# An attention and feed-forward kernel on one Trainium2 core: splitting the values by a fixed power of two, checking them by products with themselves, and judging the range early

## The chip, the cores and the metric

One core of a Trainium2 chip. The metric is the device time of one launch in microseconds. The program has five engines that run side by side and meet by semaphores: TensorE (PE, with its weight loads as PEld), VectorE (DVE), ScalarE (ACT), GpSimd (POOL) and SyncE (SP), which issues the DMAs.

## What is computed

Three steps, all from float32 inputs except the weights of the second and third, which come as float64.

```python
# 1. attention: batch 2, 8 heads, 768 positions, head size 64
scores = q @ k.T / 8 - slope[h] * dist
keep = (col < n_global) | ((0 <= row - col) & (row - col < n_local))   # 8 and 96 here
a = exp(where(keep, scores, -1e9) - max);  a = a / (sum(a) + 1e-9)
x = a @ v                                     # heads side by side: 2 x 768 x 512
# 2. h = relu(x @ w_in) (512 -> 1024), a 3-tap convolution along the positions per channel
x = (h * sigmoid(conv(h))) @ w_out            # 1024 -> 512
# 3. h = relu(x @ w_in) (512 -> 1024), u, v = halves of h; v normalised over channels
v_s = w_spatial @ v_n + b_spatial             # over the 768 positions
out = (u * v_s) @ w_out                       # 512 -> 512
```

## The kernel before, in words

Only a band of the attention is computed: 32 global columns and 96 earlier positions beside each block of 128 queries. It is right for counts within the band's reach and for numbers within the reach of float16. So the kernel computes the whole result by this banded way, gathers a flag that tells whether counts and sizes were within reach, and at its end each engine reads the flag (L1574) and branches (L1577) over a second, dense way that would compute all anew.

The positions are 6 groups (2 batches x 3 chunks of 256), each with 4 pairs of heads. A float32 operand is split into a high half (float16, scaled by a power of two, `HALF`) and a low half (what the high half left out), and a product of two such operands is three float16 matmuls: high x high, high x low, low x high (L1081 and L1151 for the second step, L1226, L1299, L1331 and L1361 for the third). In groups 0 and 1 (`PLAINS`) the values of the attention are used as they are, in float32 matmuls (L957). In groups 2 to 5 they are split: `v_scale` finds the largest absolute value of the group (`largest`, L757: a reduction over up to 1536 columns on VectorE), turns that column into a row on TensorE (L776), reduces it and makes two powers of two from its exponent in four integer steps (`scale`, L760 to L769), spreads them over the partitions by a matmul with ones (L783), and copies them out of PSUM into `cs` (L787). `v_split` then makes the high half on ScalarE (L809) and the low half on VectorE (L814), both with `cs` as a pointer operand. `weigh` uses the halves in three float16 matmuls per block (L963 to L965), and its `norm` scales back with the second power in `cs` (L969). The largest values are kept in `top`.

`watch` squares a float16 tile on ScalarE and sums it per partition into one column of `seen` (L505). Watched are x, the gated hidden blocks (`inner`, the first of 8 feature blocks of each group), ys, the weights, and the gated blocks of the third step, 61 in all. `decide` sums `seen` over the partitions with one matmul (L517), and `judge` compares each of the 61 sums with `LEAST` and `MOST`, and the largest of `top` with `MOST_X`, into the flag, in eight VectorE instructions (L526 to L533).

The order of the work is planned when the program is built. Each piece is added to `Plan` with its cost per engine it may run on, what it reads and what it writes. `order` first gives each task a time by which it is due, counted back from the end (`chain`, later `justified`), and then lists the tasks greedily (`trial`): on each engine the task that can start soonest, and of several the one that is due first; a task with two engines in its costs goes to the one that would end it sooner, within margins. PSUM banks are given out in that order too: a bank is taken at a piece's first task and comes free after its last. Six such trials are made and the shortest is taken. Each engine's instructions are then fixed in that order. A tile with fewer buffers than uses makes the later use wait for all of the earlier one (`make_room`): the raw values `v` have one buffer, their halves `vh` and `vl` two.

The lead (`tick`) goes through the steps of the attention: in the third step of a group the values of the next are loaded (`v_load`), in the sixth they are scaled, in the seventh they are split. The second step's work (`half_slot`) is added between the ticks. The third step follows (`second`), with `decide` after the last `spatial` and before the last two `last`, in the order of adding; the plan decides where they come to lie. `last` ends with evictions on ScalarE (L476) and output DMAs (L543).

Of the kernel before, what the change touches and what calls it, by code (L numbers as in the profile page):

```python
# [48 lines left out]

HALF = dict(w=8, x=11, h=12, y=12, g=12, v=8, s=16)  # L50
LEAST, MOST = 2.0e4, 4.0e9

MOST_X = 29.0

# [22 lines left out]
def dve(n):  # L77
    return 0.07 + 0.00104 * n
# [283 lines left out]
class Kernel:  # L362
    def __init__(self, ctx, tc, vb, qk, qf, kf, vf, nw, w1, cw, w2, w3u, w3v, wst, bsp, w4, out):
# [16 lines left out]
        self.craw = tile("craw", [P, 24, 2], I32)  # L380
        self.beyond = tile("beyond", [P, 4])
        self.seen = tile("seen", [P, 64])
# [3 lines left out]
        self.top = tile("top", [1, GROUPS])  # L386
        self.ng, self.nl = self.cnt[:, 0:1], self.cnt[:, 1:2]
# [21 lines left out]
            ("vl", 2 * H * D, 2), ("qk", CH + KW, 3), ("qh", CH + KW, 2), ("sb", 512, 3), ("ph", 1024, 2),  # L409
            ("pt", 1024, 2), ("xk", 2 * P, 2), ("nm", 2, 6), ("nb", 2, 6), ("r", 4, 4), ("cs", 2, 3),  # L410
            ("row", 4, 1), ("vm", 1, 1),
        )
# [98 lines left out]
    def decide(self):  # L511

        nc, n = self.nc, self.watched
        acc = self.plan.next("ps")
        self.plan.add(
            dict(PE=0.2),
            lambda e: nc.tensor.matmul(  # L517
                self.ps(acc)[:1, :n], self.column, self.seen[:, :n], start=True, stop=True
            ),
            reads=[("seen", j) for j in range(n)] + [("ident", 0)], writes=[acc],  # L520
        )

# [41 lines left out]
    def setup(self):  # L564
# [14 lines left out]
        def basics(e):  # L579
            make_identity(nc, self.ident)  # L580
            nc.gpsimd.memset(self.ones, 1.0)
            nc.gpsimd.memset(self.shift, LN2_14)
            nc.gpsimd.memset(self.column, 1.0)
            nc.gpsimd.memset(self.top, 0.0)

# [51 lines left out]
    def setup_rest(self):  # L637
# [7 lines left out]
        def flags(e):  # L645
            for j, (x, at, op) in enumerate(
                ((self.ng, float(G), ALU.is_gt), (self.nl, float(MAX_LOCAL), ALU.is_gt), (self.nl, 1.0, ALU.is_lt))
            ):
                nc.vector.tensor_scalar(
                    out=self.beyond[:, j : j + 1], in0=x, scalar1=at, scalar2=None, op0=op  # L650
                )
# [92 lines left out]

    def v_scale(self, g):
        if g in PLAINS:
            return
        nc, add = self.nc, self.plan.add
        n = 2 if g % NCH == 0 else 3
        v = self.m("v")[:, : n * 512]  # L750
        m = self.m("vm")
        row = self.m("row")[:1].bitcast(I32)
        cs = self.m("cs", g)
        top = self.top[:, g : g + 1]

        def largest(e):
            nc.vector.tensor_reduce(out=m, in_=v, axis=AX.X, op=ALU.max, apply_absolute_value=True)  # L757

        def scale(e):
            nc.vector.tensor_reduce(out=top, in_=self.ps(t)[:1, :P], axis=AX.X, op=ALU.max)  # L760
            nc.vector.tensor_scalar(
                out=row[:, 1:2], in0=top.bitcast(I32), scalar1=0x7F800000, scalar2=None, op0=ALU.bitwise_and
            )
            nc.vector.tensor_scalar(
                out=row[:, 1:2], in0=row[:, 1:2], scalar1=float(40 << 23), scalar2=-1.0,
                op0=ALU.max, op1=ALU.mult,
            )
            for j, power in ((2, 267), (3, 267 - HALF["x"])):
                nc.vector.tensor_scalar(  # L769
                    out=row[:, j : j + 1], in0=row[:, 1:2], scalar1=float(power << 23), scalar2=None, op0=ALU.add  # L770
                )

        t = self.plan.next("ps")
        add(dict(DVE=dve(n * 512)), largest, reads=[("v", g)], writes=[("vm", g)])
        add(
            dict(PE=0.12), lambda e: nc.tensor.transpose(self.ps(t)[:1, :P], m, self.ident),  # L776
            reads=[("vm", g), ("ident", 0)], writes=[t],
        )
        add(dict(DVE=0.9), scale, reads=[t, ("ident", 0)], writes=[("row", g), ("top", g)])
        t2 = self.plan.next("ps")  # L780
        add(
            dict(PE=0.05),
            lambda e: nc.tensor.matmul(self.ps(t2)[:, 0:2], self.ones, row.bitcast(F32)[:, 2:4], start=True, stop=True),  # L783
            reads=[("row", g), ("ident", 0)], writes=[t2],
        )
        add(
            dict(DVE=0.07), lambda e: nc.vector.tensor_copy(out=cs, in_=self.ps(t2)[:, 0:2]), reads=[t2],  # L787
            writes=[("cs", g)],
        )

    def v_halves(self, g):
# [3 lines left out]

    def v_split(self, g):
        if g in PLAINS:
            return
        nc, add = self.nc, self.plan.add
        cs = self.m("cs", g)  # L800
# [6 lines left out]
        def hi(e):  # L807
            if e == "ACT":
                nc.scalar.activation(out=vh, in_=v, func=AF.Copy, scale=cs[:, 0:1])  # L809
            else:  # L810
                nc.vector.tensor_scalar(out=vh, in0=v, scalar1=cs[:, 0:1], scalar2=None, op0=ALU.mult)

        def lo(e):
            nc.vector.scalar_tensor_tensor(  # L814
                out=vl, in0=v, scalar=cs[:, 0:1], in1=vh, op0=ALU.mult, op1=ALU.subtract
            )

        add(dict(ACT=act(n * 512)), hi, reads=[("v", g), ("cs", g)], writes=[("vh", g, "v")])
        add(
            dict(DVE=dve(n * 512)), lo, reads=[("v", g), ("cs", g), ("vh", g, "v")], writes=[("vl", g, "v")]  # L820
        )

# [109 lines left out]
    def weigh(self, u):  # L932
# [50 lines left out]
        )  # L983
        add(dict(DVE=1.0), norm, reads=[acc] + [("cs", g)] * (not plain), writes=[("r", u), ("xk", u)])

# [34 lines left out]
    def tick(self, more=True):  # L1020
# [5 lines left out]
        if s is not None:  # L1026
# [38 lines left out]
    def inner(self, g, f):  # L1065
# [363 lines left out]
    def banded(self):  # L1429
# [6 lines left out]
        for n in range(LEAD_TICKS):  # L1436
            if n == 2:
                self.v_scale(0)
                self.v_split(0)
# [129 lines left out]
def build(tc, *args):  # L1569
    with ExitStack() as ctx:  # L1570
        k = Kernel(ctx, tc, *args)
        k.banded()
        why = "0 or 1, whether a count or a size is beyond the reach of the banded way"
        beyond = k.nc.values_load(  # L1574
            k.flag[:1, :1], min_val=0, max_val=1, skip_runtime_bounds_check_because=why
        )
        with tc.If(beyond != 0):  # L1577
            k.dense()
# [58 lines left out]
```

## Time and profile before

| | us |
|---|---|
| median of three runs | 386.78 (386.24 to 386.82) |
| the profiled execution's own time | 385.59 |
| its span, first to last instruction | 383.7 |
| TensorE busy, share of the span | 358.4, 93% |
| VectorE busy | 277.9, 72% |
| ScalarE busy | 268.4, 70% |
| GpSimd busy | 154.7, 40% |
| mean granted clock of TensorE | 0.987 of full speed |

The profiled execution is one of the program's executions, with its own time; what a view says adds up to its span, and 1.9 us lie around that. The busy time of an engine is the union of its instructions from start to end; matmuls overlap, so the step from one start to the next tells what one costs in a stream, not its length. Branches, register reads and semaphores count as busy time nowhere, and are found under their line.

### The profile page before, as it was taken

How to read it: one execution, taken by the hardware profiler on the slowest of the kernel's cores; microseconds unless marked ns; L12 is line 12 of the kernel's file. 1: busy time of each engine (PE TensorE's matmuls, PEld its weight loads, DVE VectorE, ACT ScalarE, POOL GpSimd, SP SyncE). 2: the span in 40 equal slices, each digit the busy share in tenths (PEclk: the TensorE clock that was granted, in tenths of full speed). 3: DMA queues.
4: the chain of work that ended last, by engine and by line, in shares of the span. 5: the costliest groups of instructions: out<-in, count | busy, mean ns of one | idle time of the engine just before them, and what ended most of it. 6: DMA issues, size and time to landing. Idle time of an engine off the chain costs nothing.

```text
span 383.7 us, 7835 instructions
## 1 busy us (share of the span) xinstructions
PE 358.4 (93%) x2852; PEld 252.6 (66%) x2852; DVE 277.9 (72%) x715; ACT 268.4 (70%) x659; POOL 154.7 (40%) x225
## 2 busy tenths in 40 slices
PE   8998788789899999989899999999999999999992
PEld 5777575557778888868689766765456665555541
DVE  5799999998997899999996399881667354241501
ACT  4989797788967999898795499789947434242420
POOL 5254426895778587569653054030205100000000
PEclk9999999899999999999899999999999999999998
DMA  7979523293849557883657000450200000102021
GB/s 221 407 238 296 186 68 91 49 217 109 186 99 240 150 135 128 223 200 57 97 116 297 2 2 0 126 164 2 94 1 2 0 2 15 68 3 81 2 109 64
DMA packets 46254, 43.60 MB, mean 114 GB/s; under 512 B 34816, under 2 KB 36608, under 8 KB 45696
## 3 DMA queue, kind: packets, MB, share of 16 engines
q1 hardware_dynamic: 46208, 43.03, 40.7%
q8 instruction: 24, 0.39, 0.4%
q14 instruction: 22, 0.18, 0.1%
HBM read 31.48 MB, written 3.15 MB: 90 GB/s over the span
## 4 chain that ended last, share of the span: by engine, by line
PE 61%; DVE 21%; ACT 6%; issue 5%; DMA 3%; POOL 2%; SPq 0%; DVEq 0%; POOLq 0%
PE bank L1331 12%; PE bank L1151 10%; PE bank L1081 9%; PE bank L1299 8%; PE bank L1361 8%; PE bank L1226 8%; DVE bank L1094 4%; DVE wk_dt_float L677 3%; DVE sb_dt_float L871 3%; DVE wk_dt_float L682 2%; PE bank L852 2%; DVE wk_dt_float L674 2%; DVE ac_dt_float L1119 2%; ACT sb_dt_float L889 1%; DMA raw_dt_float<-in_w3v 1%
## 5 line engine op out<-in xcount | busy, mean ns | idle before, releaser
L1081 PE MATMUL bank<-x_dt_float,w1h_dt_float 128*128 128x260 f16 (+1 forms) x384 | 65.5, 273 | 5.7 <-DVE xk_dt_float L974 2.5
L1151 PE MATMUL bank<-hh_dt_float,w2l_dt_float 128*128 128x254 f16 (+2 forms) x192 | 53.6, 279 | 1.1 <-POOL w2l_dt_float L492 1.1
L1151 PE MATMUL bank<-hh_dt_float,w2h_dt_float 128*128 128x254 f16 (+2 forms) x192 | 53.8, 280 | 0.2 <-DVE ac_dt_float L1119 0.2
L1151 PE MATMUL bank<-hl_dt_float,w2h_dt_float 128*128 128x254 f16 (+2 forms) x192 | 53.5, 279 | 0.0
L1081 PE MATMUL bank<-x_dt_float,w1l_dt_float 128*128 128x260 f16 (+1 forms) x192 | 52.4, 273 | 0.0
L1094 DVE SCALAR_TENSOR_TENSOR bank<-hp_dt_float,cwt,bank 128x254 f32<-128x254 f32 (+2 forms) x96 | 46.2, 486 | 6.4 <-ACT bank L1088 3.6
L1331 PE MATMUL bank<-ws_dt_float,vn_dt_float 128*128 128x384 f16 x288 | 47.3, 326 | 0.0
L1081 PEld LDWEIGHTS <-w1h_dt_float 128*128 128x128 f16 x384 | 36.6, 97 | 13.2 <-issue 7.6
L492 POOL TENSOR_TENSOR hl_dt_float<-ac_dt_float,hh_dt_float 128x254 f16<-128x254 f32 (+2 forms) x47 | 33.8, 727 | 24.3 <-ACT hh_dt_float L478 21.0
L492 POOL TENSOR_TENSOR ph_dt_float<-sb_dt_float,ph_dt_float 128x512 f16<-128x512 f32 x30 | 38.4, 1283 | 11.6 <-ACT ph_dt_float L478 8.5
L1151 PEld LDWEIGHTS <-w2h_dt_float 128*128 128x128 f16 x384 | 37.0, 100 | 7.3 <-issue 0.7
L1331 PEld LDWEIGHTS <-vn_dt_float 128*128 128x128 f16 x288 | 28.2, 98 | 18.8
L871 DVE CUSTOM_DVE_ANT_0 sb_dt_float<-bank,bias_dt_float 128x256 f32<-128x256 f32 (+1 forms) x96 | 35.0, 401 | 4.7 <-POOL qk_dt_float32r L492 1.7
L889 ACT ACTIVATE sb_dt_float<-sb_dt_float,nb_dt_float 128x256 f32<-128x256 f32 (+1 forms) x64 | 29.6, 493 | 10.5 <-POOL nb_dt_float L884 9.1
L478 ACT CAST g_dt_float<-bank 128x384 f16<-128x384 f32 x16 | 7.7, 479 | 33.8 <-DVE bank L1338 33.8
L1299 PE MATMUL bank<-ys_dt_float,w3uh_dt_float 128*128 128x384 f16 x128 | 31.2, 326 | 0.0
L1335 DVE SCALAR_TENSOR_TENSOR bank<-bank,bb_dt_float 128x384 f32<-128x384 f32 x16 | 9.1, 567 | 29.1 <-PE bank L1331 29.1
L1361 PE MATMUL bank<-w4h_dt_float,g_dt_float 128*128 128x512 f16 (+1 forms) x104 | 28.8, 363 | 0.0
L1226 PE MATMUL bank<-w3vh_dt_float,ys_dt_float 128*128 128x512 f16 x96 | 28.6, 379 | 0.0
L1361 PEld LDWEIGHTS <-g_dt_float 128*128 128x128 f16 x156 | 15.2, 98 | 15.8
L677 DVE SCALAR_TENSOR_TENSOR wk_dt_float<-raw_dt_float,wk_dt_float 128x512 int32<-128x512 int32 x28 | 24.9, 898 | 0.1
L1226 PEld LDWEIGHTS <-ys_dt_float 128*128 128x128 f16 x144 | 14.1, 98 | 15.6
(172 smaller groups left out, 894.0 us busy)
## 6 DMA issues: line engine op xcount, KB each, us to landing
raw_dt_float<-in_w SPq DMA_DIRECT2D x20, 512.0 KB, 5.4
qk_dt_float<-in_qk SPq DMA_DIRECT2D x24, 336.0 KB, 3.9
v_dt_float<-in_vb SPq DMA_DIRECT2D x4, 1024.0 KB, 5.7
out_x<-wk_dt_float SPq DMA_DIRECT2D x11, 256.0 KB, 2.0
raw_dt_float<-in_wst SPq DMA_DIRECT2D x6, 384.0 KB, 4.4
raw_dt_float<-in_w3v SPq DMA_DIRECT2D x4, 512.0 KB, 5.2
raw_dt_float<-in_w3u SPq DMA_DIRECT2D x4, 512.0 KB, 6.3
v_dt_float<-in_vb SPq DMA_DIRECT2D x2, 768.0 KB, 5.9
```

Source lines behind the costliest of these rows:

```text
L492: self.engines[e].tensor_tensor(out=out, in0=in0, in1=in1, op=ALU.subtract)
L677: nc.vector.scalar_tensor_tensor(out=fi, in0=lo, scalar=29, in1=fi, op0=ALU.logical_shift_right, op1=ALU.bitwise_or)
L871: nc.vector.tensor_tensor_reduce(out=sb[:, h, :n], in0=self.ps(self.sp[s][h])[:, :n], in1=self.m("bias", 2 * p + h)[:, t0 : t0 + n], scale ...
L889: nc.scalar.activation(out=sb[:, h, :n], in_=sb[:, h, :n], func=AF.Exp, scale=-1.0, bias=nb[:, h : h + 1])
L1081: nc.tensor.matmul(self.ps(acc)[:, :nx], w[f][:, k * P : (k + 1) * P], x[:, k, x0:], start=k == n == 0, stop=k == 3 and n == 2,)
L1094: nc.vector.scalar_tensor_tensor(out=ac(), in0=near(j), scalar=tap(j), in1=ac(), op0=ALU.mult, op1=ALU.add)
L1151: nc.tensor.matmul(ps(), w[2 * d + k // 4][:, k % 4 * P : (k % 4 + 1) * P], x, start=k == n == 0, stop=k == 7 and n == 2,)
L1226: nc.tensor.matmul(ps(), x[:, y, k, tk], w[k], start=n == 0, stop=n == 11)
L1299: nc.tensor.matmul(ps(), w[e4][:, k * P : (k + 1) * P], x[:, y, k, s], start=n == 0, stop=n == 11)
L1331: nc.tensor.matmul(ps(), v[:, k, x, ek], w[:, k, s], start=n == 0, stop=n == 17)
L1335: nc.vector.scalar_tensor_tensor(out=ps(), in0=ps(), scalar=2.0 ** -(self.k["v"] + self.k["s"]), in1=bb, op0=ALU.mult, op1=ALU.add)
L1361: nc.tensor.matmul(ps(), x[:, y, k, tk], w[k][:, at], start=n == 0, stop=n == 11)
```

## The change

`v_scale` goes, with its call and its tiles `cs`, `row`, and `top`. `v_split` uses the same helper as all other splits (`parts`), with the fixed power of two of `HALF["x"]`, now 9 in place of 11: the high half may go to ScalarE or VectorE, the low half to VectorE. A new `watch_values` multiplies each 128 x 128 block of the high half with itself on TensorE, 12 blocks in group 3 and 16 in groups 2, 4 and 5, all summed in one PSUM bank, and takes the diagonal with the identity on VectorE, summed into a column of `seen`. `norm` has constants for both of its scalars. The gated hidden blocks are watched in the first chunk of each batch alone, twice in place of six times, so that `seen` has 61 columns as before. `judge` has four instructions instead of eight, its planned cost is 6.0 us in place of 1.0, and the flag has the opposite sense.

```diff
-HALF = dict(w=8, x=11, h=12, y=12, g=12, v=8, s=16)
+HALF = dict(w=8, x=9, h=12, y=12, g=12, v=8, s=16)
...
         def judge(e):
-            sums, fit, top = self.ps(acc)[:1, :n], self.m("vm")[:1], self.top
-            good = self.m("junk")[:1, :n]
+            sums, good = self.ps(acc)[:1, :n], self.m("junk")[:1, :n]
             nc.vector.tensor_scalar(out=good, in0=sums, scalar1=LEAST, scalar2=None, op0=ALU.is_ge)
             nc.vector.scalar_tensor_tensor(out=good, in0=sums, scalar=MOST, in1=good, op0=ALU.is_le, op1=ALU.mult)
-            nc.vector.tensor_reduce(out=fit, in_=good, axis=AX.X, op=ALU.min)
-            nc.vector.tensor_scalar(out=self.beyond[:1, 3:4], in0=fit, scalar1=0.5, scalar2=None, op0=ALU.is_lt)
-            nc.vector.tensor_reduce(out=fit, in_=top, axis=AX.X, op=ALU.max)
-            nc.vector.tensor_scalar(out=fit, in0=fit, scalar1=MOST_X, scalar2=None, op0=ALU.is_gt)
-            nc.vector.tensor_tensor(out=self.beyond[:1, 3:4], in0=self.beyond[:1, 3:4], in1=fit, op=ALU.max)
-            nc.vector.tensor_reduce(out=self.flag[:1], in_=self.beyond[:1], axis=AX.X, op=ALU.max)
+            nc.vector.tensor_reduce(out=self.within[:1, 3:4], in_=good, axis=AX.X, op=ALU.min)
+            nc.vector.tensor_reduce(out=self.flag[:1], in_=self.within[:1], axis=AX.X, op=ALU.min)
...
-        self.plan.add(
-            dict(DVE=1.0), judge, reads=[acc, ("flag", 0)] + [("top", g) for g in range(GROUPS)],
-            writes=[("junk", 0), ("vm", GROUPS)],
-        )
+        self.plan.add(dict(DVE=6.0), judge, reads=[acc, ("flag", 0)], writes=[("junk", 0)])
...
-        add(dict(ACT=act(n * 512)), hi, reads=[("v", g), ("cs", g)], writes=[("vh", g, "v")])
-        add(
-            dict(DVE=dve(n * 512)), lo, reads=[("v", g), ("cs", g), ("vh", g, "v")], writes=[("vl", g, "v")]
-        )
+        self.parts(n * 512, vh, vl, v, [("v", g)], [("vh", g, "v")], [("vl", g, "v")], 2.0 ** HALF["x"])
+        self.watch_values(g, vh, n * NPAIR)
+
+    def watch_values(self, g, vh, n):
...
+        at = self.watched
+        self.watched += 1
+        acc = self.plan.next("ps")
+
+        def products(e):
+            for j in range(n):
+                self.nc.tensor.matmul(
+                    self.ps(acc)[:, :P], vh[:, j], vh[:, j], start=j == 0, stop=j == n - 1
+                )
+
+        def diagonal(e):
+            self.nc.vector.tensor_tensor_reduce(
+                out=self.ps(acc)[:, P : 2 * P], in0=self.ps(acc)[:, :P], in1=self.ident, scale=1.0, scalar=0.0,
+                op0=ALU.mult, op1=ALU.add, accum_out=self.seen[:, at : at + 1],
+            )
+
+        self.plan.add(dict(PE=0.055 * n), products, reads=[("vh", g, "v")], writes=[acc])
+        self.plan.add(dict(DVE=0.35), diagonal, reads=[("ident", 0)], writes=[acc, ("seen", at)])
...
-                out=r, in0=op[:, :, 0 : VW : VW - 1], scalar1=1.0e-9 if plain else 1.0e-9 * 2.0**14,
-                scalar2=2.0 ** -HALF["x"] if plain else self.m("cs", g)[:, 1:2], op0=ALU.add, op1=ALU.mult,
+                out=r, in0=op[:, :, 0 : VW : VW - 1], scalar1=2.0 ** -HALF["x"] if plain else 1.0,
+                scalar2=1.0e-9 * 2.0 ** (-HALF["x"] if plain else 14), op0=ALU.mult, op1=ALU.add,
...
-                if s % 8 == 5:
-                    self.v_scale(g)
...
-        if f == 0:
+        if f == 0 and c == 0:
             self.watch(hh, nout, [("hh", n, "h")])
...
-        with tc.If(beyond != 0):
+        with tc.If(within == 0):
             k.dense()
```

## Rows read from the trace of the kernel before

**Rows 1.** Stretches: us, busy us of each engine (x instructions), granted clock, DMA.
```profile
80.00:120.00 40.00, 36.72 (x399) 29.76 (x398) 35.01 (x113) 33.32 (x83) 29.60 (x45) 1.00 0.67 165
120.00:160.00 40.00, 40.00 (x435) 32.70 (x434) 35.97 (x107) 35.21 (x84) 27.76 (x41) 1.00 0.72 169
160.00:200.00 40.00, 36.38 (x399) 30.13 (x397) 38.83 (x104) 35.10 (x94) 27.86 (x37) 0.96 0.61 114
200.00:376.00 176.00, 176.00 (x1125) 108.09 (x1122) 94.68 (x179) 99.59 (x242) 27.96 (x36) 1.00 0.16 56
```

**Rows 2.** TensorE's waits from 80 to 200 us: total us, times, longest.
```profile
PE bank L1005 <- DVE xk_dt_float L974: 2.4, 2, 1.8
...
PE bank L776 <- DVE vm_dt_float L757: 1.0, 1, 1.0
```

**Rows 3.** VectorE groups by shape: xcount, busy us, mean ns, idle before.
```profile
L757 DVE TENSOR_REDUCE vm_dt_float<-v_dt_float 128x1 f32<-128x1536 f32 x3 | 5.2, 1749 | 0.1
L871 DVE CUSTOM_DVE_ANT_0 sb_dt_float<-bank,bias_dt_float 128x160 f32<-128x160 f32 x16 | 4.6, 320 | 1.7 <-POOL qk_dt_float32r L492 1.7
...
L969 DVE TENSOR_SCALAR r_dt_float<-bank,cs_dt_float 128x4 f32<-128x4 f32 x16 | 3.4, 212 | 0.0
...
L969 DVE TENSOR_SCALAR r_dt_float<-bank 128x4 f32<-128x4 f32 x8 | 1.2, 153 | 1.6 <-PE bank L957 1.6
...
L760 DVE TENSOR_REDUCE top<-bank 1x1 f32<-1x128 f32 x4 | 1.1, 271 | 0.0
...
L769 DVE TENSOR_SCALAR row_dt_float<-row_dt_float 1x1 int32<-1x1 int32 x8 | 0.8, 136 | 0.1
L787 DVE COPY cs_dt_float<-bank 128x2 f32<-128x2 f32 x4 | 0.6, 155 | 0.6 <-PE bank L783 0.6
...
L761 DVE TENSOR_SCALAR row_dt_float<-top 1x1 int32<-1x1 int32 x4 | 0.6, 141 | 0.1
```

**Rows 4.** TensorE in time order, around 107 and 109 us.
```profile
107.18 0.27 PE L1151 MATMUL bank<-hh_dt_float,w2l_dt_float 128*128 128x256 f16 x1
107.29 0.27 PE L776 MATMUL bank<-ident,vm_dt_float 128*1 128x128 f32 x1
107.40 0.27 PE L1151 MATMUL bank<-hh_dt_float,w2h_dt_float 128*128 128x256 f16 x1
...
109.14 0.27 PE L1151 MATMUL bank<-hh_dt_float,w2l_dt_float 128*128 128x256 f16 x1
109.35 0.38 PE L783 MATMUL bank<-row_dt_float,ones 1*128 1x2 f32 x2
109.66 0.28 PE L1151 MATMUL bank<-hh_dt_float,w2h_dt_float 128*128 128x256 f16 x1
```

**Rows 5.** TensorE in order of time, twelve narrow matmuls and their successor.
```profile
130.57 0.20 PE L963 MATMUL bank<-vh_dt_float,pt_dt_float 128*128 128x65 f16 x1
...
130.94 0.27 PE L1081 MATMUL bank<-x_dt_float,w1h_dt_float 128*128 128x260 f16 x1
```

**Rows 6.** The end: chain, last eviction, SyncE wait for the flag, L1577.
```profile
360.66 15.57 PE bank L1361 x84
376.23 0.21 PE bank L517 x2
...
377.91 0.14 DVE flag L533
...
376.32 0.38 ACT L476 ACTIVATE wk_dt_float<-bank 128x256 f32<-128x256 f32 x1 [0.93 <-PE bank L1361]
...
SPq L1574 <- DVE flag L533: 1.0, 1, 1.0
...
L1577 SPq EVENT_SEMAPHORE  x8: 17/17/17, 379.1 to 379.7; - x8
...
L1577 PEldq COMPARE_BRANCH  x1: 3909/3909/3909, 378.7 to 378.7; - x1
...
L1577 ACTq EVENT_SEMAPHORE  x1: 17/17/17, 381.7 to 381.7; - x1
```

More of the change, by code (lines that the diff above doesn't have):

```diff
@@ L46 @@
 BIASES = 2
-HALF = dict(w=8, x=11, h=12, y=12, g=12, v=8, s=16)
+HALF = dict(w=8, x=9, h=12, y=12, g=12, v=8, s=16)
 LEAST, MOST = 2.0e4, 4.0e9
-MOST_X = 29.0
 ROUNDS, SLACK, AHEAD, MARGIN, BIAS, CLOSE = 6, 0.5, 30.0, 1.0, 10.0, 15.0
@@ L380, in __init__ @@
         self.craw = tile("craw", [P, 24, 2], I32)
-        self.beyond = tile("beyond", [P, 4])
-        self.seen = tile("seen", [P, 64])
+        self.within = tile("within", [P, 4])
+        self.seen = tile("seen", [P, 72])
         self.column = tile("column", [P, 1])
@@ L385, in __init__ @@
         self.few = tile("few", [P, G])
-        self.top = tile("top", [1, GROUPS])
         self.ng, self.nl = self.cnt[:, 0:1], self.cnt[:, 1:2]
@@ L409, in __init__ @@
             ("vl", 2 * H * D, 2), ("qk", CH + KW, 3), ("qh", CH + KW, 2), ("sb", 512, 3), ("ph", 1024, 2),
-            ("pt", 1024, 2), ("xk", 2 * P, 2), ("nm", 2, 6), ("nb", 2, 6), ("r", 4, 4), ("cs", 2, 3),
-            ("row", 4, 1), ("vm", 1, 1),
+            ("pt", 1024, 2), ("xk", 2 * P, 2), ("nm", 2, 6), ("nb", 2, 6), ("r", 4, 4), ("vm", 1, 1),
         )
@@ L583, in basics @@
             nc.gpsimd.memset(self.column, 1.0)
-            nc.gpsimd.memset(self.top, 0.0)
         add(dict(POOL=0.9), iotas, writes=[("keep", 0)])
@@ L646, in flags @@
             for j, (x, at, op) in enumerate(
-                ((self.ng, float(G), ALU.is_gt), (self.nl, float(MAX_LOCAL), ALU.is_gt), (self.nl, 1.0, ALU.is_lt))
+                ((self.ng, float(G), ALU.is_le), (self.nl, float(MAX_LOCAL), ALU.is_le), (self.nl, 1.0, ALU.is_ge))
             ):
                 nc.vector.tensor_scalar(
-                    out=self.beyond[:, j : j + 1], in0=x, scalar1=at, scalar2=None, op0=op
+                    out=self.within[:, j : j + 1], in0=x, scalar1=at, scalar2=None, op0=op
                 )
@@ L743, in ones_beside @@
         self.plan.add(dict(POOL=0.15), lambda e: self.nc.gpsimd.memset(out, 1.0), writes=[name])
[L745 to L762, printed above, removed]
-            )
[L764 to L774, printed above, removed]
-        add(
[L776 to L789, printed above, removed]
     def v_halves(self, g):
@@ L798, in v_split @@
             return
-        nc, add = self.nc, self.plan.add
-        cs = self.m("cs", g)
         n = 3 if g % NCH == 0 else 4
@@ L805, in v_split @@
         vh, vl = vh[:, : n * NPAIR, 1 : 1 + 2 * D], vl[:, : n * NPAIR]
[L807 to L815, printed above, removed]
-            )
-        add(dict(ACT=act(n * 512)), hi, reads=[("v", g), ("cs", g)], writes=[("vh", g, "v")])
-        add(
-            dict(DVE=dve(n * 512)), lo, reads=[("v", g), ("cs", g), ("vh", g, "v")], writes=[("vl", g, "v")]
-        )
+        self.parts(n * 512, vh, vl, v, [("v", g)], [("vh", g, "v")], [("vl", g, "v")], 2.0 ** HALF["x"])
[13 more added lines that the diff above has]
+                op0=ALU.mult, op1=ALU.add, accum_out=self.seen[:, at : at + 1],
+            )
+        self.plan.add(dict(PE=0.055 * n), products, reads=[("vh", g, "v")], writes=[acc])
+        self.plan.add(dict(DVE=0.35), diagonal, reads=[("ident", 0)], writes=[acc, ("seen", at)])
     def qk_load(self, u):
@@ L983, in weigh @@
         )
-        add(dict(DVE=1.0), norm, reads=[acc] + [("cs", g)] * (not plain), writes=[("r", u), ("xk", u)])
+        add(dict(DVE=1.0), norm, reads=[acc], writes=[("r", u), ("xk", u)])
     def x_parts(self, g):
@@ L1437, in banded @@
             if n == 2:
-                self.v_scale(0)
                 self.v_split(0)
@@ L1572, in build @@
         k.banded()
-        why = "0 or 1, whether a count or a size is beyond the reach of the banded way"
-        beyond = k.nc.values_load(
+        why = "0 or 1, whether counts and sizes are within the reach of the banded way"
+        within = k.nc.values_load(
             k.flag[:1, :1], min_val=0, max_val=1, skip_runtime_bounds_check_because=why
         )
-        with tc.If(beyond != 0):
+        with tc.If(within == 0):
             k.dense()
```

## The prediction, before the changed kernel had run

> **What bounds the kernel now.** I read the stretches first, then TensorE's own waits, then VectorE's groups by shape, and last the end of the span. In the stretches [rows 1] the reader sees two regimes. From 200 to 376 us TensorE is busy without a gap (176.00 of 176.00), so there only TensorE's work counts. From 80 to 200 us, where the four later groups of the attention run and the change has its edits, TensorE is idle for 3.28, 0.00 and 3.62 us in the three stretches, 6.9 us in all, while VectorE is 88, 90 and 97% busy. The waits name the releaser [rows 2]: the longest is the normalised block xk of VectorE (2.4 us); one, 1.0 us, is the transpose inside the scale chain, which waits for that chain's own reduction. All but that one are VectorE coming late with something else, 6.6 us over the seven rows of that view, so 5.6 us without it. The granted clock is 1.00, 1.00 and 0.96: a little of the third stretch runs at the lower of the two levels (1.2 in place of 2.4 GHz). The stretch is limited by TensorE with VectorE close behind, and both sides of the change must be weighed: it takes work from VectorE and gives some to TensorE.
>
> **The scale chain goes: VectorE.** Per later group it is one reduction over the values, one over a row, four tiny integer steps and a copy. Over four groups the busy sums are 5.2 for three reductions and 5.2 / 3 x 2 / 3 = 1.2 for the fourth (1024 columns, not 1536), 1.1 for the row, 0.6 each for the first two integer steps (the second, L764, is like L761), 0.8 for the other two and 0.6 for the copy: 10.1 us [rows 3]. The normalisation's first step loses its pointer operand: 16 times 212 ns become the 153 ns of the plain groups' form, 0.9 us less [rows 3]. Added are four diagonals of 128 columns out of PSUM with an accumulated sum. The nearest row is the masked minimum with its accumulator over 160 columns, 320 ns [rows 3]; I take 0.3 us each, 1.2 us. Net, VectorE loses 9.8 us, or 8% of the 120 us.
>
> **The scale chain goes: TensorE.** The transpose delays its successor by 0.11 us (107.29 to 107.40), and the broadcast with ones by 0.41 us (109.14 to 109.66, where 256 columns alone step by 0.11, as 107.18 to 107.29) [rows 4]. Four of each are 2.1 us. The wait of 1.0 us [rows 2] has no instruction left to wait in.
>
> **The products come: TensorE.** Four groups bring 16 + 12 + 16 + 16 = 60 products of 128x128 by 128 columns in f16, each with a weight load of its own. The trace has no such shape. Twelve matmuls of 64 or 65 columns, also each with its own load, take 130.57 to 130.94, 31 ns each [rows 5]; 256 columns step by 110 ns [rows 4]. A line between the two gives 56 ns at 128 columns and 3.4 us for 60; the bounds are 31 and 110 ns, or 1.9 and 6.6 us. I take 56 because both ends lie on one straight line of time against columns.
>
> The rows therefore show that a stream of narrow matmuls with their own loads runs at 31 ns. The Trainium skill (TensorE: Matmul & The Clock Gate, section Back-to-back issue gap) says that such pairs sustain about 81 ns at 128 columns. By that rule the 60 would cost an estimated 4.9 us, 1.5 us more than my sum; the trace, at less than half of it for 65 columns, speaks against taking it.
>
> So TensorE's own work between 80 and 200 us is 3.4 - 2.1 = 1.3 us more, and 1.0 us of waiting goes.
>
> **What the lighter VectorE gives back.** This is the uncertain term: 5.6 us of TensorE's waiting is for VectorE, bounds 0 and 5.6. The 160 to 200 us stretch, with VectorE 97% busy [rows 1], is where it is plainly late; the decodes of weights that fill it have no early deadline and can move into the room that the chain leaves earlier. At 80 to 120 us the waits stand beside 5 us of VectorE idling, so there order matters more than load. I take half, 2.8 us. What is late next is then TensorE itself.
>
> **New waits.** Each diagonal waits on VectorE for its products, with the rest of VectorE's planned order behind it, and the weighing and the scores behind that. Before, the chain had two such waits per group; the copy's came to 0.6 us [rows 3]. One replaces two, so I set it at nothing; if TensorE runs late against the order, each could cost that 0.6 us again. A PSUM bank is held from the first product to the diagonal, where the chain held two in turn. The high half may now be given to VectorE as well as ScalarE: nothing if it stays, and by the reduction's rate [rows 3] some 2.3 us a group if not; that is a rival below.
>
> **Fewer squares.** Four of the six squares of the gated blocks go from ScalarE. No wait of TensorE from 80 to 200 us is ended by ScalarE (of the seven rows all name VectorE), so I take nothing; it can only give ScalarE room for the high halves.
>
> **The end.** The last output products run 360.66 to 376.23, the column sum follows, then eight VectorE steps to the flag at 378.05 [rows 6]. All engines read the flag, branch over the other path, and only then finish. TensorE's branch starts at 378.7 and takes 3909 ns, to 382.6; ScalarE goes on at 381.7 [rows 6], and the span ends at 383.7, 1.1 us after TensorE's branch. The rows thus charge the branch, not the judging, with most of the end. With a planned cost of 6 us for the judging instead of 1, column sum and judging are due 6 us before the end, and the data for them exist once the last gated block is squared, soon after 360.66. So the flag is ready before the last products, and each engine reads it when its own work is done. TensorE's last product starts at about 376.2, the column sum (0.21 us) now lying ahead of it. It branches 0.65 us after it may (378.05 to 378.7 now): 376.2 + 0.65 + 3.9 + 1.1 = 381.9, or 1.8 us earlier than 383.7. ScalarE's route is 376.7 (its last eviction) + 3.7 + 1.1 = 381.5, so TensorE decides. Bounds: SyncE, the last to have work, waited 1.0 us for the flag [rows 6], so at least 1.0 us is saved if it is ready. At most 3.8 us, if the other engines' branches are hidden and SyncE's own list of semaphores ends last: it ends 1.7 us after the flag now (379.7), so 377.05 + 1.7 + 1.1 = 379.9.
>
> **The sum** is 1.3 - 1.0 - 2.8 - 1.8 = -4.3 us. The profiled execution took 385.59 us (span 383.7 and 1.9 around it), 1.2 us below the median of the three runs shown, 386.78. Against the median that is 382.5.
>
> **The rivals.**
> *TensorE is the bound, nothing comes back.* The waits of 5.6 us stay, since the planned order is anew a greedy list and VectorE may get the high halves (9 us, all of its relief). Against: 160 to 200 us has VectorE at 97%. Then 1.3 - 1.0 - 1.8 = -1.5: 385.3 us. Chance 0.26.
> *The flag is not early.* The change does not do there what it says, because the column sum still ends up behind the last products on TensorE; for it speaks that it is a filler with nobody waiting but the judging. Then only four of the eight steps between 376.44 and 378.05 go, about 0.7 us: 1.3 - 1.0 - 2.8 - 0.7 = -3.2, 383.6 us. Chance 0.09.
> *The products run at the rate of 256 columns, and it gets slower.* One mechanism: the same tile is both stationary and moving, in rows of 130 halves that begin at the second, so each pair may step by 110 ns instead of 56. It costs 6.6 us in a stretch without slack at 120 to 160 us. With the waits unchanged: 6.6 - 2.1 - 1.0 - 1.8 = +1.7, 388.5 us. It decides from 82 ns per product on (60 x 82 ns = 4.9 us, against 2.1 + 1.0 + 1.8). Against it: the weighing reads the same tile as moving data at 31 ns. Chance 0.12.
> The forecast itself has 0.53.
>
> **The numbers.** The likeliest is 382.5. Its own bounds (waits 0 to 5.6, end 1.0 to 3.8, products 1.9 to 6.6) do not fall together; I let it reach 3 us down, 379.6, and up to 387.0, which takes in both faster rivals and leaves out most of the slow one. A measurement of this kernel can tell about 0.2%, 0.8 us. Faster is the forecast, the flag's rival and most of the bound's rival: 0.77. Same takes the part of that rival and of the slow one that lies within 0.8 us: 0.12. Slower is the rest of the slow one and a poorer order: 0.11.
>
> **What would show it.** Right: the 60 products in 3 to 4 us; TensorE idle from 80 to 200 us near 3 us, not 7; VectorE busy 98 to 101 us there, not 109.8; the flag written more than 3 us before TensorE's last product; and from the end of the last products to the span's end under 6 us, where it is 7.5 now (376.23 to 383.7). Wrong: products stepping by 80 ns or more, TensorE idle as before with VectorE lighter, or a flag written after the last eviction.

## The result, and the profile after

The changed kernel takes **381.88 us** (median; 380.87 to 382.52), the kernel before beside it 386.80 (386.24 to 387.25): ratio **0.987, 95% interval 0.985 to 0.9895**. That is 0.6 us below the forecast of 382.5 and inside its range. The profiled execution took 380.87 us, with a span of 379.2 us, 4.5 us shorter than before (383.7).

One boundary splits these 4.5 us. The spatial step is one unbroken run of TensorE work, and its first product started at 298.2 us before. From there to the end of the span it is 85.5 us before. A source line's rows (count; min, median and max ns; first and last start) give that start, first in the kernel before and then in the kernel after:

```profile
L1331 PE MATMUL bank<-ws_dt_float,vn_dt_float x288: 326/326/326, 298.2 to 360.3; 128*128 128x384 f16 x144
```
```profile
core 0 of [0], span 379.2 us
engine op xcount: duration ns min/median/max, first and last start us, forms
...
L1278 PE MATMUL bank<-ws_dt_float,vn_dt_float x288: 326/326/326, 296.5 to 358.7; 128*128 128x384 f16 x144
```

So 1.7 us were won ahead of it (298.2 to 296.5) and 379.2 - 296.5 = 82.7 us remain behind it, 2.8 less. These two numbers, the *start* and the *end part*, are what I compare in the experiments. Both come from one profiled execution of each kernel, and the section on f1 shows that the start of an unchanged order can move by 1.3 us from one execution to another.

**The attention, 80 to 200 us.** The stretches of the kernel after, as [rows 1]:

```profile
80.00:120.00 40.00, 37.18 (x427) 29.93 (x424) 32.60 (x102) 34.72 (x79) 27.11 (x35) 0.99 0.69 172
120.00:160.00 40.00, 39.93 (x445) 32.92 (x443) 31.20 (x95) 32.88 (x82) 26.70 (x41) 1.00 0.59 130
160.00:200.00 40.00, 38.38 (x430) 32.14 (x429) 37.41 (x108) 37.76 (x102) 26.96 (x37) 1.00 0.62 127
```

TensorE is idle for 2.82, 0.07 and 1.62 us, 4.5 in all, where it was 6.9. VectorE is busy for 101.2 us, where it was 109.8. Ahead of 80 us, before the first chain (83.7 us in the kernel before) or the first product (85.9 us after) begins, TensorE is idle for 9.4 us, where it was 11.1. What TensorE still waits for there (total us, times, longest), as [rows 2]:

```profile
PE bank L954 <- DVE xk_dt_float L923: 2.9, 3, 1.3
PE bank L1098 <- POOL hl_dt_float L488: 0.8, 1, 0.8
PE bank L912 <- DVE nm_dt_float L820: 0.5, 1, 0.5
PE bank L912 <- DMA pt_dt_float<-ph_dt_float: 0.2, 1, 0.2
```

The wait on the chain's own reduction (1.0 us) has gone with the chain. The normalised block xk is late as before (2.9 us, 2.4 before), though its engine has 8.6 us less to do.

**The products.** TensorE in order of time in the kernel after, the first later group with its successor, and then VectorE's groups by shape for the normalisation's first step and the diagonal, as [rows 3]:

```profile
85.86 1.10 PE L759 MATMUL bank<-vh_dt_float 128*128 128x128 f16 x16
86.80 0.38 PE L1028 MATMUL bank<-x_dt_float,w1h_dt_float 128*128 128x260 f16 x2
```
```profile
L918 DVE TENSOR_SCALAR r_dt_float<-bank 128x4 f32<-128x4 f32 x24 | 3.6, 152 | 1.2 <-PE bank L914 1.2
...
L764 DVE CUSTOM_DVE_ANT_0 bank<-bank,ident 128x128 f32<-128x128 f32 x4 | 1.2, 293 | 0.1
...
L764 DVE DVE_READ_ACCUMULATOR2_ANT seen<- 128x1 f32 x4 | 0.6, 140 | 0.0
```

Sixteen products hold TensorE from 85.86 to 86.80, 58.5 ns each, so 60 take 3.5 us. The printed 1.10 us is no guide: it runs to the modelled end of the last one, and successors start earlier. A diagonal is 293 ns and a second instruction of 140 ns that reads out the sum, 1.8 us for four.

**The end.** The flag, who loads it and when, and the branch, in the kernel after, as [rows 6] (three source lines):

```profile
L524 DVE TENSOR_REDUCE flag<-within x1: 145/145/145, 365.2 to 365.2; 1x1 int32<-1x4 f32 x1
...
L1520 POOLq TENSOR_LOAD <-flag x1: 738/738/738, 365.4 to 365.4; - x1
L1520 DVEq TENSOR_LOAD <-flag x1: 803/803/803, 365.4 to 365.4; - x1
L1520 PEldq TENSOR_LOAD <-flag x1: 492/492/492, 372.8 to 372.8; - x1
L1520 ACTq TENSOR_LOAD <-flag x1: 465/465/465, 375.0 to 375.0; - x1
L1520 SPq TENSOR_LOAD <-flag x1: 519/519/519, 375.8 to 375.8; - x1
...
L1523 SPq EVENT_SEMAPHORE  x8: 17/17/17, 376.9 to 377.4; - x8
...
L1523 PEldq COMPARE_BRANCH  x1: 3639/3639/3639, 373.4 to 373.4; - x1
L1523 ACTq COMPARE_BRANCH  x1: 50/50/50, 375.6 to 375.6; - x1
L1523 SPq COMPARE_BRANCH  x1: 53/53/53, 376.4 to 376.4; - x1
...
L1523 ACTq EVENT_SEMAPHORE  x1: 17/17/17, 378.2 to 378.2; - x1
```

The last output product starts in the row below, of TensorE's order of time:

```profile
374.65 0.27 PE L1308 MATMUL bank<-w4l_dt_float,g_dt_float 128*128 128x256 f16 x1
```

The flag is there 9.3 us before that product starts. TensorE loads it at 372.8 and begins its branch at 373.4, while its own last products have yet to start: the branch of 3.6 us is over at 377.1, and it lies beside products, eviction and store. ScalarE, which has to evict the last block first, goes on at 378.2 and is what the span then ends with. From the end of the last products (374.9) it is 4.3 us to the end, where it was 7.5.

### The profile page after: what moved, and what is told of

It is laid out like the page before. It is cut to its first block, busy times and chain, and to the rows that moved or that the text cites. A ratio compares the mean times of both kernels' runs of the same rounds, so it can differ in the third digit from the quotient of the medians.

```text
span 379.2 us, 7892 instructions
## 1 busy us (share of the span) xinstructions
PE 360.5 (95%) x2893; PEld 254.7 (67%) x2893; DVE 271.5 (72%) x695; ACT 265.4 (70%) x650; POOL 156.3 (41%) x221
## 4 chain that ended last, share of the span: by engine, by line
PE 51%; DVE 25%; ACT 11%; issue 6%; POOL 3%; DMA 2%; DVEq 0%; POOLq 0%; ACTq 0%
PE bank L1278 12%; PE bank L1308 8%; PE bank L1246 8%; PE bank L1098 6%; DVE wk_dt_float L665 5%; PE bank L1173 5%; DVE bank L1041 5%; DVE wk_dt_float L670 4%; DVE sb_dt_float L820 3%; PE bank L801 3%; PE bank L1028 3%; DVE wk_dt_float L662 3%; DMA pt_dt_float<-ph_dt_float 2%; ACT sb_dt_float L838 2%; PE bank L999 1%
## 5 line engine op out<-in xcount | busy, mean ns | idle before, releaser
L1098 PE MATMUL bank<-hh_dt_float,w2h_dt_float 128*128 128x254 f16 (+2 forms) x192 | 53.0, 276 | 0.0
L488 POOL TENSOR_TENSOR hl_dt_float<-ac_dt_float,hh_dt_float 128x256 f16<-128x256 f32 (+2 forms) x44 | 32.6, 747 | 33.5 <-ACT hh_dt_float L474 28.8
L488 POOL TENSOR_TENSOR ph_dt_float<-sb_dt_float,ph_dt_float 128x512 f16<-128x512 f32 x29 | 36.6, 1264 | 18.7 <-ACT ph_dt_float L474 16.7
L662 DVE TENSOR_SCALAR wk_dt_float<-wk_dt_float 128x512 int32<-128x512 int32 x28 | 18.6, 673 | 8.5 <-ACT wk_dt_float L655 8.4
```

Of the source, the lines that this page charges most:

```text
L488: self.engines[e].tensor_tensor(out=out, in0=in0, in1=in1, op=ALU.subtract)
L662: nc.vector.tensor_scalar(out=fi, in0=fi, scalar1=3, scalar2=None, op0=ALU.logical_shift_left)
L1098: nc.tensor.matmul(ps(), w[2 * d + k // 4][:, k % 4 * P : (k % 4 + 1) * P], x, start=k == n == 0, stop=k == 7 and n == 2,)
```

## Experiments

Four questions: is it the early flag that shortens the end; what is the scale chain worth; what do the products cost; and how much of the rest is the planner's order? Kernels planned anew mix each edit with a new order. So all the kernels named f keep a known order piece by piece, and apart from their edit their instructions follow one another on every engine as in the kernel they come from. The ratio is always to runs of the kernel before made beside them (f1 to f4 beside one series of it, f5, f6, e7 and the repetition beside another, e1 to e4 beside a third). The result of all the runs, with the two numbers from the profile:

| kernel | median us | ratio to before [95%] | start | end part |
|---|---|---|---|---|
| before | 386.09 to 386.80 | | 298.2 | 85.5 |
| after | 381.88 | 0.987 [0.985, 0.9895] | 296.5 | 82.7 |
| after, again | 381.47 | 0.987 [0.985, 0.990] | 295.9 | 83.1 |
| e1 late judge | 382.08 | 0.988 [0.9855, 0.991] | 295.0 | 84.8 |
| e2 early judge alone | 386.18 | 0.998 [0.995, 1.0005] | 301.3 | 82.5 |
| f1 early judge, old order | 383.79 | 0.9915 [0.989, 0.994] | 299.5 | 82.5 |
| f2 e1's order, judge moved | 379.72 | 0.982 [0.980, 0.9845] | 294.7 | 82.8 |
| f3 chain out, old order | 384.30 | 0.995 [0.993, 0.997] | 296.2 | 85.5 |
| e3 no products, planned anew | 384.12 | 0.991 [0.988, 0.995] | 299.6 | 82.6 |
| f4 products out, new order | 384.65 | 0.994 [0.9915, 0.997] | 299.1 | 82.5 |
| f5 products twice, new order | 384.56 | 0.995 [0.993, 0.997] | 299.7 | 82.7 |
| e4 dead reduction, planned anew | 383.52 | 0.992 [0.989, 0.995] | 300.0 | 82.6 |
| f6 dead reduction, new order | 383.43 | 0.992 [0.9895, 0.995] | 298.2 | 83.1 |
| e7 planned anew | 388.53 | 1.0055 [1.003, 1.008] | 303.1 | 83.1 |

### The end: e1, e2, f1, f2

e1 is the kernel after with the old planned cost of the judging, e2 the kernel before with the new one:

```diff
-        self.plan.add(dict(DVE=6.0), judge, ...    # e1, in after
+        self.plan.add(dict(DVE=1.0), judge, ...
-            dict(DVE=1.0), judge, ...              # e2, in before
+            dict(DVE=6.0), judge, ...
```

> The changed kernel, the judging's planned cost 1.0 us again in place of 6.0; nothing else. Theory A (the end was shortened because the flag is ready before the last products, so that the engines read it and branch one by one): the flag comes last again; the distance from TensorE's last output product to the span's end goes from 4.5 us back towards 7.0 (the judging keeps its four steps), so 2.0 to 3.0 us slower than the changed kernel, 384 to 385 us. Rival (the shorter judging and the work before 376 us made the gain): under 0.8 us slower. Two further engines' branches, of VectorE and GpSimd, should then start within 0.2 us of TensorE's.

> The kernel before with one number changed: the judging's planned cost 6.0 us in place of 1.0, all eight steps kept. Theory A: the end alone gives 2.7 to 3.3 us, so 383.5 to 384.1 us against 386.8, and the rest of the changed kernel's 4.9 us is the scale chain's. Rival (early judging only pays with the short judging, or the end is bound by the last output's DMA): within 0.8 us of the kernel before.

Measured: e1 382.08 us, e2 386.18. Both totals missed what theory A expected and lie where the rival had them. But neither tells anything by itself, since each plan came out in another order; the two parts do. In e2 the end part falls from 85.5 to 82.5 us, and the start comes 3.1 us later, which eats it. In e1 the end part is 84.8, with 7.0 us from the last output product to the end as expected, and the start comes 1.5 us earlier than in the kernel after. There the flag is written at 374.0, behind the last product, and all five engines wait for it (the branch's source line in e1):

```profile
L1523 SPq EVENT_SEMAPHORE  x8: 17/17/17, 375.3 to 375.9; - x8
L1523 ACTq COMPARE_BRANCH  x1: 50/50/50, 374.8 to 374.8; - x1
...
L1523 PEldq COMPARE_BRANCH  x1: 3462/3462/3462, 374.9 to 374.9; - x1
L1523 ACTq EVENT_SEMAPHORE  x1: 17/17/17, 378.3 to 378.3; - x1
L1523 PEldq EVENT_SEMAPHORE  x1: 51/51/51, 378.4 to 378.4; - x1
```

The branch starts together everywhere and its 3.5 us on TensorE are at the end again. The shorter decision alone is thus worth 0.7 us (85.5 to 84.8), the early flag 2.1 (84.8 to 82.7). Once the flag is early, the shorter decision adds nothing: e2, with all eight steps, has 82.5.

f1 and f2 keep an order and move only the column sum and the judging, by hand: f1 in the order of before, f2 in that of e1.

```diff
+    def earlier(self, order):
+
+        judge = next(i for i, t in enumerate(self.tasks) if t[1].__name__ == "judge")
+        moved = [x for x in order if x[0] in (judge - 1, judge)]
+        rest = [x for x in order if x[0] not in (judge - 1, judge)]
+        at = [j for j, x in enumerate(rest) if x[1] == "PE"][-4]
+        return rest[:at] + moved + rest[at:]
...
-        order = self.order()
+        order = self.earlier(self.order())
```

> The kernel before in its own order on every engine; only the column sum on TensorE, and with it the judging (all eight steps), is moved by hand ahead of the last four output pieces. Theory A (the end is shortened by 3.0 us from the first product of the spatial step to the span's end, 85.6 to 82.6 us as in the trace of the judging planned early, and what that kernel lost elsewhere is its changed order in the attention): 383.2 to 384.0 us. Rival (judging early gains nothing that lasts, because the engines' branches collide with the last transfers): 386 us or more.

> The changed kernel planned with the judging at 1.0 us, and then the column sum and judging moved by hand ahead of the last four output pieces: the order of the late-judge run but for this one move. Theory A with order luck (that run's attention reached the spatial step 1.5 us earlier than the changed kernel, and lost 2.2 us at the end): 379.5 to 380.3 us, better than both kernels. Rival (the earlier attention of that run was a matter of one execution): 381.5 us or more.

Measured: f1 383.79 us, 2.6 below the 386.37 beside it, and its end part is 82.5. f2 379.72 us, **the fastest kernel of the study**, with e1's early start (294.7) and the short end (82.8). Where e1 has 374.9, f1 shows TensorE's branch ahead of SyncE's and ScalarE's turn:

```profile
L1585 SPq EVENT_SEMAPHORE  x8: 17/17/17, 379.8 to 380.4; - x8
...
L1585 PEldq COMPARE_BRANCH  x1: 4052/4052/4052, 376.3 to 376.3; - x1
L1585 ACTq COMPARE_BRANCH  x1: 50/50/50, 378.5 to 378.5; - x1
...
L1585 ACTq EVENT_SEMAPHORE  x1: 17/17/17, 381.1 to 381.1; - x1
```

With the order kept, an early flag gives 2.6 us of the median and 3.0 us of the end part; f2 against e1 gives 2.4 and 2.0. This part of the explanation is shown.

f1 also shows what the start of one execution is worth. Up to the moved pieces its program is that of before, and yet its start is 1.3 us later (299.5). The stretch from 70 to 82 us, before and in f1:

```profile
70.00:82.00 12.00, 11.45 (x78) 8.10 (x78) 11.93 (x28) 8.44 (x21) 10.36 (x10) 0.86 0.62 146
```
```profile
70.00:82.00 12.00, 11.46 (x55) 8.27 (x56) 11.32 (x23) 7.72 (x19) 10.35 (x9) 0.57 0.67 161
```

The granted clock of 0.57 in place of 0.86 means some 10 us at the lower level (1.2 GHz) in place of 3, and 55 matmuls in place of 78. A start that differs by little more than 1 us therefore needs the medians beside it.

### The scale chain: f3

The order of before, the chain's five pieces emit nothing, and the scale is set once:

```diff
+                nc.gpsimd.memset(self.m("cs", g)[:, 0:1], 2.0**15)
+                nc.gpsimd.memset(self.m("cs", g)[:, 1:2], 2.0**4)
...
+        largest = scale = none = lambda e: None
         add(dict(DVE=dve(n * 512)), largest, reads=[("v", g)], writes=[("vm", g)])
```

> The kernel before in its own order, but the scale chain's five pieces emit nothing: the two powers of two are written once at the start, so the values are split by a constant. No scale is found. Theory B (TensorE limits the attention's stretch with VectorE close behind, so 2.1 us of TensorE's steps, 1.0 us of waiting and part of the other 5.6 us go): 381 to 383.4 us. Rival (the chain lay beside other work): within 0.8 us of the kernel before. A middle result, 383.5 to 385, would say that TensorE's steps count and VectorE's relief does not.

Measured: 384.30 us, 2.1 below before; the start 2.0 us earlier, the end part unchanged at 85.5. Its stretches:

```profile
80.00:120.00 40.00, 36.12 (x398) 29.67 (x397) 30.91 (x99) 33.43 (x83) 30.13 (x45) 1.00 0.68 166
120.00:160.00 40.00, 38.82 (x427) 31.73 (x425) 33.45 (x96) 36.12 (x85) 25.29 (x42) 1.00 0.75 174
160.00:200.00 40.00, 37.27 (x420) 30.88 (x419) 38.80 (x105) 35.45 (x96) 28.44 (x38) 1.00 0.59 117
```

This is the middle result that the expectation named. VectorE is at 103.2 us where it was at 109.8, and TensorE idles for *more*: 3.88 + 1.18 + 2.73 = 7.8 us against 6.9, although the wait of 1.0 us inside the chain is gone. So TensorE gained its own steps and that wait (2.1 + 1.0 by the prediction), and its other waits grew by 1.9 us. The relief of VectorE gave nothing back in this order. Part of the earlier start is the clock's: the third stretch ran at 1.00 here and at 0.96 before [rows 1]. The matmul that starts at 185.96 us before starts 1.8 us earlier in f3, that at 189.90 us 3.4 us earlier, and from 207.99 us on it is 1.9. How much of the 2.1 us of the median is the chain's and how much the clock's, no run divides.

### The products: e3, f4, f5

e3 leaves the call out and plans anew; f4 keeps the order and emits neither products nor diagonals; f5 keeps the order and issues each product twice.

```diff
-        self.watch_values(g, vh, n * NPAIR)                     # e3
...
+        products = diagonal = lambda e: None                    # f4
+            nc.gpsimd.memset(self.seen, 1000.0)
...
             for j in range(n):                                  # f5
+                for twice in range(2):
```

> The changed kernel without the products of the values with themselves and their diagonals: the values' range is not examined. It has 3.5 us less for TensorE (60 products at 58.5 ns in the changed kernel's trace). Theory (TensorE limits the attention's stretch, so the products are paid for): 2 to 3.5 us faster than the changed kernel, 378.5 to 380 us. Rival (they fill gaps in which TensorE waits for VectorE): within 0.8 us.

> The changed kernel in its own order, but products and diagonals emit nothing; the values' range is not examined. It has 3.5 us less for TensorE and 1.7 us less for VectorE. Theory B: 2.8 to 4 us faster than the changed kernel, about 378.5 us. Rival (the products lie in gaps in which TensorE would wait for VectorE anyway): within 0.8 us, 381 us or more. The replanned kernel without products, at 384.1 us, would then be slow through its order alone.

> The changed kernel in its own order, each of the 60 products done twice: 3.5 us more for TensorE, in the same four places. Theory C (at these places TensorE runs ahead of VectorE and would wait soon after, so the products cost little): under 1 us slower than the changed kernel, 381.5 to 383 us. Rival B (TensorE's own work sets the time there): 3 to 4 us slower, 385 to 386 us.

Measured: e3 384.12 us, f4 384.65 and f5 384.56. Twice the products cost 3.1 us against the 381.47 beside it, as rival B expected and close to 60 x 58.5 ns = 3.5. By that price no products at all should have given 3.5 us, but f4's ratio lies above that of the kernel after, by some 3 us, which no theory expected. Even its two executions with the highest mean clock (0.987) took 382.14 and 382.54 us, no less than the kernel after. e3 tells little: its order is new, and its profiled execution had a mean clock of 0.968, where the kernel after had 0.984. TensorE's waits from 80 to 200 us in f4:

```profile
PE bank L945 <- DVE xk_dt_float L914: 4.3, 4, 2.1
PE bank L903 <- DMA pt_dt_float<-ph_dt_float: 2.6, 3, 1.2
PE bank L1089 <- POOL hl_dt_float L488: 1.0, 2, 0.8
PE bank L903 <- DVE nm_dt_float L811: 0.8, 1, 0.8
```

Set beside the four rows of the kernel after, they grew from 4.4 to 8.7 us, by more than the products' 3.5: what TensorE does not spend on products it spends waiting for VectorE's blocks and for the transposing transfer. The matmul that starts at 77.21 us in the kernel after starts at 78.28 in f4, and that at 200.05 starts at 202.60. So 1.1 us of f4's loss lie ahead of 80 us and 1.5 in the attention's stretch itself. Ahead of it, f4's stretch from 24 to 34 us, and the same of the kernel after:

```profile
24.00:34.00 10.00, 9.86 (x40) 7.55 (x42) 9.21 (x30) 6.16 (x18) 4.30 (x6) 0.50 0.75 221
```
```profile
24.00:34.00 10.00, 8.65 (x46) 6.03 (x46) 9.44 (x30) 6.82 (x19) 3.88 (x6) 0.66 0.75 240
```

A granted clock of 0.50 is the lower level (1.2 GHz) for the whole stretch; 40 matmuls get through there instead of 46. f4 is also 0.7 us late already behind its first scores, at 7.6 us; f1 is 0.5 us late at the same place with no edit there, so this need not be f4's edit. What f4 shows is that leaving the products out gained nothing in the stretch they were taken from; why that stretch even took 1.5 us longer stays open.

### VectorE's load: e4, f6

Both add a reduction of 1536 columns per group (in e4 1024 for one of the four) whose result nobody reads. e4 plans it at its cost; f6 keeps the order and puts it right behind the diagonal.

```diff
+        self.plan.add(dict(DVE=dve((n - 1) * 512)), largest, reads=[("v", g)], writes=[("vm", g)])   # e4
...
+            self.nc.vector.tensor_reduce(                       # f6, in diagonal()
+                out=self.m("vm"), in_=self.m("bias", 0)[:, :256].unsqueeze(1).to_broadcast([P, 6, 256]),
```

> The changed kernel with the old reduction over the values put back, four times on VectorE, 6.4 us in all, its result read by nobody. Theory (the lighter VectorE lets TensorE wait less): 1 to 2.5 us slower than the changed kernel, 383 to 384.4 us. Rival (what helped was that the chain's own steps on TensorE and its waits went, and VectorE has room): within 0.8 us.

> The changed kernel in its own order, with a reduction over 1536 columns on VectorE right behind each of the four diagonals, read by nobody: about 7 us more for VectorE. Theory C (TensorE waits for VectorE after each of these places, so VectorE's work is what counts): 2 to 5 us slower than the changed kernel, 384 to 387 us. Rival B (VectorE has room): under 0.8 us slower.

Measured: e4 383.52 us, f6 383.43, 2.0 above the 381.47 beside it. In f6 the addition is this group:

```profile
L768 DVE TENSOR_REDUCE vm_dt_float<-bias_dt_float 128x1 f32<-128x1536 f32 x4 | 7.0, 1747 | 0.0
```

7.0 us on VectorE cost 2.0 us of time, the least that theory C expected. A longer VectorE does matter in the new order, though it is only 84% busy between 80 and 200 us.

### The order: e7 and the kernel after again

The same program planned anew, with the products' planned cost at the measured 58.5 ns instead of 55:

```diff
-        self.plan.add(dict(PE=0.055 * n), products, reads=[("vh", g, "v")], writes=[acc])
+        self.plan.add(dict(PE=0.0585 * n), products, reads=[("vh", g, "v")], writes=[acc])
```

> The changed kernel with nothing but the planned cost of a product changed, 0.0585 us as the trace has it in place of 0.055; the program does the same work, in another order. If the order alone moves the time: up to 2 us to either side of the changed kernel, its end unchanged (82.6 us from the first product of the spatial step). Rival (orders of the same work are worth the same): within 0.5 us.

> The changed kernel once more, beside the three: its runs give the spread that the others are held against; 381 to 382.6 us as before.

Measured: the kernel after again 381.47 us, e7 **388.53 us**, slower than the kernel before and far beyond the 2 us that were expected of the order. The work is the same; only the planner's order, and its choice of engine for a few copies, differ. The better price made the plan worse by 7.1 us, and VectorE, in all, is 6.4 us busier (277.9 against 271.5). Where TensorE waits from 80 to 200 us in e7:

```profile
PE bank L954 <- DVE xk_dt_float L923: 5.0, 3, 2.5
PE bank L1098 <- POOL hl_dt_float L488: 1.9, 2, 1.4
PE bank L801 <- DVE nm_dt_float L820: 1.1, 2, 0.7
PE bank L912 <- DVE nm_dt_float L820: 1.0, 1, 1.0
```

9.0 us instead of 4.4 in the rows, but the longest one, 2.5 us, ends at 80.10 us and lies almost wholly ahead of the stretch: within it TensorE is idle for 6.9 us, where the kernel after again has 4.0. Up to the spatial step TensorE is idle for 18.4 us against 14.1, which is 4.3 of the 7.2 us by which e7's start is later; in the other 2.9 it is longer busy with the same work. The end part is that of the kernel after again (83.1).

## Why the prediction came out right, point by point

- **Products, +3.4.** Right in size: 58.5 ns each, 3.5 us. The line between the narrow matmuls and those of 256 columns [rows 4, 5] held; it gives 57 ns at 128 columns where I wrote 56, which leaves the sum at 3.4. By the Trainium skill (TensorE: Matmul & The Clock Gate, Back-to-back issue gap), such pairs would take about 81 ns at 128 columns; the trace disagrees. The rival at 110 ns falls with it.
- **Chain on TensorE, -2.1, and its wait, -1.0.** The steps and the wait are gone. But in f3 other waits grew by 1.9 us, so that more than half of the two terms' 3.1 came back as waiting; the start of its profile, 2.0 us earlier, holds a gain of the clock besides.
- **What the lighter VectorE gives back, -2.8.** The step that was sized too large. TensorE's idle time fell by 2.4 us (6.9 to 4.5) where the prediction had 3.8 with the chain's wait, so 1.4 of the 2.8 came. And the mechanism is not shown: with the order of before, f3's relief brought nothing, while f6's load in the new order cost 2.0. The 1.4 us belong to load and order together, and no run divides them.
- **The end, -1.8.** The other mis-sized term, by 1.0 us: it measured -2.8 in the kernel after and -3.0 in f1 and e2, between the forecast and its bound of 3.8. The step that failed is "TensorE decides": I let its branch begin after its last product, while its queue loads the flag and branches 1.3 us before that product starts. ScalarE ends last instead, at 378.2.
- **The rivals.** "The flag is not early" is refuted by the flag at 365.2. "TensorE is the bound, nothing comes back" is refuted in its total (385.3), but f3 shows its core for the order of before.
- **The signs.** Products, flag and end came as said (3.5 us; 9.3 us ahead; 4.3 us). TensorE's idle time of 4.5 us lies between the 3 of "right" and the 7 of "wrong", and VectorE's 101.2 just above the 98 to 101.
- **New waits and the high halves, nothing.** The high halves stayed on ScalarE. VectorE fell by 8.6 us where 9.8 was predicted; the accumulator's second instruction, 0.6 us, is part of the difference.
- **Fewer squares, nothing.** Not tried by itself.

So the sum was near because two misses nearly cancel, and that is luck: 1.0 us too little at the end, and 0.8 too much ahead of it, where 2.5 us were forecast (1.0 + 2.8 - 1.3) and 1.7 came. The first rests on runs in kept orders. The second is less sure: f1's start moved by 1.3 us without an edit, and by the medians some 2.3 us are left beside f1's 2.6 (386.80 - 381.88 = 4.9). Nor did the 1.7 us come as the prediction had them. The products' 3.5, the chain's -2.1 and the 2.4 us of idle time make only -1.0; ahead of 80 us, where no edit acts yet, TensorE idles for 9.4 us in place of 11.1. The 1.7 us ahead of the spatial step are the new order's as much as the edits': e7 has every edit, and its start comes 4.9 us later than that of before (303.1 against 298.2). Added up across the kept orders, f1's 2.6 and f3's 2.1 less f5's 3.1 make 1.6 of the 4.9 us; to what the other 3.3 belong no run shows, and e7 moved by 7.1 through its order alone. That TensorE alone bounds 80 to 200 us, as I read it, is half the truth: f5 (more TensorE work costs almost all of itself) and f6 (more VectorE work costs a part) show both engines near the path, and in f4, with the products gone, the waits for VectorE and for a transfer took their place.

## What to carry to other kernels

Where two engines wait for each other in turn, a cost taken off one need not be worth its duration, though the same cost added may be, as f4 and f5 show for the products; try both directions in a kept order. With a list planner, compare edits in one order and treat the order as a variable of its own: a 6% change of one planned cost moved this kernel by 7 us, more than the whole change. Read a gain of 1 or 2 us from medians, not from one profile. And put a decision that every engine branches on far ahead of the last work: here VectorE, GpSimd and TensorE then paid their branches beside that work, and only the engines with the last work, ScalarE and SyncE, paid theirs at the end.

## What the runs showed of the hardware

- **A branch costs TensorE 3.5 to 4.1 us.** 3909 ns before, 3639 in the kernel after, 3462 in e1, 3649 in e2 and 4052 in f1. ScalarE's goes on 2.6 us after its own (375.6 to 378.2 after), SyncE's 0.5 us after. The Trainium skill (Runtime: NRT & Kernel Launch, Instruction fetch mechanics) says that a taken branch out of the fetched window has to fetch its target first; the rows agree with a stall of that kind but don't show a fetch, and the page gives no size.
- **TensorE's queue runs ahead of its array.** It loads the flag at 372.8, 1.9 us before the last product that stands ahead of the load has started (374.65).
- **The same program spreads by 0.8% in time.** Before ranged from 385.66 to 388.85 us beside f1 to f4. In the profiles, stretches at the lower clock differ from kernel to kernel, as f4's above, and between executions of the same work, as f1's from 70 to 82 us (0.57 in place of 0.86).
